# First loads shared between two DMA queues, a prefetch hint for the closing branch, and the last store as one: a softcap attention and feed-forward kernel on one core

## The chip, the cores and the metric

One core of a Trainium2 chip runs the whole kernel. The metric is the device time in microseconds (us) of one execution. A core has TensorE (PE in the rows; its weight loads are PEld), VectorE (DVE), ScalarE (ACT), GpSimd (POOL) and SyncE (SP), which run their own streams of instructions and wait for each other by semaphores. DMAs (copies between the chip's main memory and the on-chip memory) are issued here by SP, ACT and POOL. An engine's letter followed by q (SPq, ACTq) is its sequencer: it issues DMAs, waits, loads registers and branches.

## The reference

```python
def _attn_ref(q, k, v, cap) -> np.ndarray:
    scale = 1.0 / np.sqrt(q.shape[-1])
    scores = scale * np.matmul(q, k.transpose(0, 1, 3, 2))
    scores = cap * np.tanh(scores / cap)
    scores = scores - np.max(scores, axis=-1, keepdims=True)
    attn = np.exp(scores)
    attn = attn / (np.sum(attn, axis=-1, keepdims=True) + 1e-09)
    return np.matmul(attn, v).astype(np.float32)

def _moe_ref(x, w_in, w_out) -> np.ndarray:
    h = x @ w_in
    g = h - np.tanh(h)
    return (g @ w_out).astype(np.float32)
```

q, k and v have 4 batches, 12 heads, 448 rows and 64 columns; the weights are 768 x 2048 and 2048 x 768 and arrive as 64-bit floats. The 1792 x 768 attention result is the input x of the second function.

## The kernel before

The heads are taken in pairs (24 of them: 4 batches times 6). For each pair the kernel loads k and q, transposes them on DVE (L552), splits them into a high and a low part whose products give the precision of 32-bit floats, multiplies on PE (L736 for the first 8 pairs, L701 for the rest), takes tanh and exp on ACT (L746, L709, L801), multiplies with v (L880 and after) and normalises (L912 to L953). The feed-forward part goes over 16 slices of 128 hidden columns: the 64-bit weights are decoded on DVE, split, and used by PE (L1213 to L1215 for the first matrix, L1266 for the second). The last columns of the last rows come in `rest` (L1364 to L1366).

No order is written out by hand. `Build` records each operation with its engine, a cost and a due time in a `Plan`; `Plan.schedule` then plays the program through with these costs and always takes the operation that can start first. `START` holds the times at which PE, ACT, DVE, SP and POOL become free in that play, so it shifts choices all through the order. Copies that ACT or DVE could do (engine "AD") are given out on the way. `Plan.run` tries three settings and emits the instructions in the order of the best.

The places that the change and the prediction touch:

- `softcap_attention_ffn` (L1548): loads `cap`, makes `warm`, a one-element tile, and runs a tanh on it (L1556), which loads ACT's table at the start. Then it builds the main program, loads a flag into a register of every engine (L1575), and branches (L1576): a second, general program stands behind `tc.If(fv == 0)`. With these inputs the flag is 1, so that the general program is jumped over.
- `warm_up` (L474): 18 matmuls on zeros, ahead of the first scores.
- `fetch_qk` (L488): four DMAs for each of k and q, all on SP's queue (L499).
- `fetch_v` (L513): of its two forms, L531 reads a source that stands twice, `tail.unsqueeze(0).to_broadcast([2, TAIL, D])`, so that its outer dimension is 2, into 128 partitions.
- `put` (L1473): stores a tile of results (L1487). The last tile, `fel`, holds rows of two batches, and is stored in halves of 64 partitions. Its last 256 columns, copied out of PSUM last of all, go out in two DMAs, one on SP's queue and one on ACT's.

At the very end SP waits for the landing of every DMA, one semaphore after another, and a barrier of all engines closes the program (L1608).

Of the kernel before, what the change touches and what calls it, by code (L numbers as in the profile page):

```python
# [14 lines left out]
AF = mybir.ActivationFunctionType  # L15
# [35 lines left out]

URGENT = 1000.0

START = (1700.0, 2000.0, 3300.0, 1060.0, 2300.0)
SETTINGS = [(0.0, 0.0), (0.0, 200.0), (0.0, 500.0)]

LAT, LAT_PE, DMA_START, DMA_END = 140.0, 200.0, 650.0, 1100.0
# [34 lines left out]
class Plan:  # L92
# [177 lines left out]
                return c  # L270
        return None

    def run(self, settings):
        best = min((self.schedule(*s) for s in settings), key=lambda r: r[0])
        for o, e in best[1]:
            for b in o.alloc:
                b.tile = self.make(b)
            if o.eng == "AD":
                o.fn(e)
            else:  # L280
                o.fn()
# [33 lines left out]
class Build:  # L315
# [6 lines left out]
    def __init__(self, ctx, tc, q, k, v, w_in, w_out, out, consts, checks, general):  # L322
        self.tc, self.nc = tc, tc.nc
        nc = self.nc
        self.q, self.k, self.v, self.w_in, self.w_out, self.out = q, k, v, w_in, w_out, out
        self.general = general
        self.absc, self.s8 = consts
        self.B, self.H, self.S, self.D = q.shape
        self.NP = self.H // 2
        self.DM, self.DFF = w_in.shape  # L330
        self.ND = self.DM // 128
        self.NF = self.DFF // 128
        self.FULL = self.S // 128 * 128
        self.TAIL = self.S - self.FULL
        B, S, D = self.B, self.S, self.D
        nm = self.nm = "g" if general else "f"
        self.cst = ctx.enter_context(tc.tile_pool(name=nm + "cst", bufs=1))
        self.sb = ctx.enter_context(tc.tile_pool(name=nm + "sb", bufs=2))
        self.ps = ctx.enter_context(tc.tile_pool(name=nm + "ps", bufs=1, space=PSUM))
        self.dram = ctx.enter_context(tc.tile_pool(name=nm + "dram", bufs=1, space=bass.MemoryType.DRAM))  # L340
        self.u_kept = [self.dram.tile([128, 2, self.DM], F32, name=f"{nm}uk{f}") for f in range(self.NF)]
        self.uid = 0
        self.plan = Plan(self.make)
        for name, n in self.sizes().items():
            self.plan.tag(name, n)

        self.fixed = {"kst": [], "kz": [], "kt": [], "vraw": []}  # L350
        S = self.S
        for i in range(self.plan.tags["kst"]):
            t = self.cst.tile([128, 2 * S + self.TAIL], F32R, name=f"{nm}kst{i}")
            nc.gpsimd.memset(t.bitcast(F32)[:, S : S + self.TAIL], 0.0)
            self.fixed["kst"].append(t)


        for i in range(self.plan.tags["kz"]):
            t = self.cst.tile([128, 2 * S], F32R, name=f"{nm}kz{i}")
            nc.gpsimd.memset(t.bitcast(F32)[D:, 0:S], 0.0)  # L360
            nc.gpsimd.memset(t.bitcast(F32)[:D, S:], 0.0)
            self.fixed["kz"].append(t)
        for i in range(self.plan.tags["kt"]):
            t = self.cst.tile([128, 2, 2, self.TAIL], F32R, name=f"{nm}kt{i}")
            nc.gpsimd.memset(t.bitcast(F32)[:D, :, 1, :], 0.0)
            nc.gpsimd.memset(t.bitcast(F32)[D:, :, 0, :], 0.0)
            self.fixed["kt"].append(t)
        self.v1s = {F32: [], F32R: []}
        for i in range(self.plan.tags["vraw"]):
            t = self.cst.tile([128, 4, 2, D], F32, name=f"{nm}vraw{i}")  # L370
            self.fixed["vraw"].append(t)
        tail = B * self.TAIL
        self.xt = [self.cst.tile([128, tail], F32, name=f"{nm}xt{d}") for d in range(self.ND)]
        self.x, self.xt_ops = {}, {d: [] for d in range(self.ND)}
        self.raw_qk, self.ready, self.raw_v = {}, {}, {}
        self.raw, self.u, self.w, self.kept_op = {}, {}, {}, {}
        self.segments = [(m, a, z) for m, a, z in SEGMENTS]
        later = {m for m, a, _ in self.segments if a}
        self.x_kept = {
            m: [self.dram.tile([128, 2, self.FULL], F32, name=f"{nm}xk{m}_{d}") for d in range(self.ND)] for m in later  # L380
        }
        self.y_kept = {
            m: [self.dram.tile([128, self.DM], F32, name=f"{nm}yk{m}_{i}") for i in range(3)] for m in later
        }
        self.x_ops, self.y_ops = {}, {}
        self.acc = {}
        self.at = 0.0
        if not general:
            self.least, self.flagf, self.flag = checks
            self.seen = self.cst.tile([128, 2, self.NF], F32, name="seen")  # L390
            self.ok = self.cst.tile([128, 2, self.NF], F32, name="ok")
            self.bad = self.cst.tile([128, 2], F32, name="bad")
            self.seen_ops = []
# [80 lines left out]
    def warm_up(self):  # L474

        nc, P = self.nc, self.plan.buf("s")
        z = self.plan.buf("xh", [128, self.FULL], F32R)

        def fn():
            for _ in range(WARM):  # L480
                nc.tensor.matmul(P()[:, : self.FULL], z()[:, 0:128], z(), start=True, stop=True)

        o = self.plan.op("D", 300.0, lambda: nc.vector.memset(z().bitcast(F32), 0.0), [], [z], key=-1e6)
        self.plan.op("PE", COLS[384] * WARM, fn, [o], [P], [z], key=-1e6)

    def fetch_qk(self, b, p, np_):  # L488

        nc, S = self.nc, self.S  # L490
        for nm, src in (("k", self.k), ("q", self.q)):
            raw = self.plan.buf(nm + "raw", [128, 2, S // 32, 32])
            ops = []
            for i in range(4):
                hp, dh = divmod(i, 2)
                h = p + self.NP * hp

                def fn(i=i, h=h, dh=dh, raw=raw, src=src):
                    nc.sync.dma_start(  # L499
                        out=raw()[32 * i : 32 * i + 32, 0:np_],  # L500
                        in_=src[b, h : h + np_].rearrange("h (j b) (i a) -> i b h j a", b=32, a=32)[dh],
                    )

                ops.append(
                    self.dma("SP", np_ * S * 128, fn, [], [] if ops else [raw], [raw] if ops else [], slow=2.3)
                )
            for j in range(np_):
                self.raw_qk[nm, b, p + j] = (raw, j, ops)
# [964 lines left out]
    def put(self, i, m, o, deps, cols):  # L1473
        nc, S, T = self.nc, self.S, self.TAIL
        if i < 3:
            r = S * m + 128 * i
            parts = [(slice(0, 128), self.out[r : r + 128, cols])]
        else:

            tails = self.out.rearrange("(b s) c -> b s c", s=S)[2 * (i - 3) : 2 * (i - 3) + 2, self.FULL :, cols]  # L1480
            parts = [(slice(T * j, T * j + T), tails[j]) for j in range(2)]
        for n, (rows, out) in enumerate(parts):

            eng = "A" if i == 4 and n and cols.start else "SP"
            self.dma(
                eng, (rows.stop - rows.start) * (cols.stop - cols.start) * 4,
                lambda q=nc.scalar if eng == "A" else nc.sync, rows=rows, out=out: q.dma_start(  # L1487
                    out=out, in_=o()[rows, cols]
                ),
                deps, [], [o], key=self.at + 20000,  # L1490
            )


    def emit(self):
# [21 lines left out]
        done, b = 0.0, 0  # L1516
# [4 lines left out]
        for c in gen:  # L1521
            if isinstance(c, tuple):
                if c[1] == NP - 1:
                    done, b = 0.0, c[0] + 1
# [8 lines left out]
        done, k = 0.0, 0  # L1533
        self.at = starts[0]
        for c in self.moe():
# [5 lines left out]
                self.at = starts[k] + done * (starts[k + 1] - starts[k]) / own[k]  # L1541
            else:
                self.at = starts[k] + done
        self.plan.run(SETTINGS[:1] if self.general else SETTINGS)


@with_exitstack
def softcap_attention_ffn(ctx: ExitStack, tc: tile.TileContext, q, k, v, cap, w_in, w_out, out):  # L1548
    nc = tc.nc
    cpool = ctx.enter_context(tc.tile_pool(name="consts", bufs=1))  # L1550
    c = cpool.tile([128, 1], F32, name="capt")
    nc.sync.dma_start(out=c, in_=cap.to_broadcast([128, 1]))

    warm = cpool.tile([1, 1], F32, name="warm")
    nc.vector.memset(warm, 0.0)
    nc.scalar.activation(warm, warm, AF.Tanh)  # L1556
    neg = cpool.tile([128, 1], F32, name="negc")
    nc.vector.tensor_scalar_mul(neg, c, -1.0)

    absc = cpool.tile([128, 1], F32, name="absc")  # L1560
# [3 lines left out]
    s8 = cpool.tile([128, 1], F32, name="s8")  # L1564
# [2 lines left out]
    nc.vector.tensor_scalar(flagf, absc[0:1], CAP_BOUND, None, op0=ALU.is_le)  # L1567
    least = cpool.tile([128, 1], F32, name="least")
    nc.vector.memset(least, F64_MIN)
    args = (q, k, v, w_in, w_out, out, (absc, s8), (least, flagf, flag))  # L1570
    with ExitStack() as es:
        build = Build(es, tc, *args, general=False)
        es.enter_context(tc.manual_schedule())
        build.emit()
    fv = nc.values_load(flag[0:1, 0:1], min_val=0, max_val=1)  # L1575
    with tc.If(fv == 0):  # L1576
        with ExitStack() as es:
            build = Build(es, tc, *args, general=True)
            es.enter_context(tc.manual_schedule())
            build.emit()  # L1580
# [32 lines left out]
```

## Time and profile before

| what | us |
|---|---|
| median of 3 runs (lowest, highest) | 705.78 (705.69, 705.79) |
| the profiled execution | 704.82 |
| its span, from the first to the last instruction | 703.0 |
| PE busy in the span | 686.1 |
| ACT busy | 535.6 |
| DVE busy | 520.5 |
| POOL busy | 21.9 |

The profiled execution is one run, recorded by the hardware; its span leaves out 1.82 us that lie around the first and last instruction. Busy time counts an engine's computing instructions, not its sequencer's. Start times in rows count from the start of the span.

### The profile page before, as it was taken

To read this page: it belongs to the slowest core of one execution; us is meant where nothing else is said; L and a number is where in the kernel's file an instruction comes from. 1 tells how busy PE (TensorE), PEld (TensorE's weight loads), DVE (VectorE), ACT (ScalarE), POOL (GpSimd) and SP (SyncE) were. 2 spreads that over 40 slices of the span, in tenths; PEclk is the share of its full clock that TensorE was granted. 3 is DMA by queue.
4 is the path that set the end of the run, shared out by engine and by line. 5 is a ranking of instruction groups with operands and counts; after the bars stand their busy time and mean duration, and the time that the engine had idled before them with its cause. 6 is when DMAs were issued, how large, how long until landed. Compare 5 with 4: busy or idle time off the path is not lost.

```text
span 703.0 us, 10228 instructions
## 1 busy us (share of the span) xinstructions
PE 686.1 (98%) x3672; PEld 587.7 (84%) x3672; DVE 520.5 (74%) x799; ACT 535.6 (76%) x925; POOL 21.9 (3%) x51
## 2 busy tenths in 40 slices
PE   8999999999999999999999999999999999999995
PEld 6445677777889998899989888989999999999995
DVE  4889998999887889998799789798784334333431
ACT  6988878788896959498888998899785555555454
POOL 2011100000000000000000000000000000000000
PEclk9999999999999999999999999999999999999998
DMA  7999999999954646799576865577569544566513
GB/s 107 162 226 243 280 252 243 212 238 260 192 201 147 132 133 188 262 198 323 191 162 190 259 183 149 173 202 217 156 175 269 166 126 135 159 180 179 142 39 118
DMA packets 159520, 133.06 MB, mean 189 GB/s; under 512 B 115748, under 2 KB 144036, under 8 KB 159460
## 3 DMA queue, kind: packets, MB, share of 16 engines
q1 hardware_dynamic: 156308, 117.30, 66.5%
q0 software_dynamic: 3072, 14.94, 5.9%
q8 instruction: 31, 0.51, 0.3%
q14 instruction: 29, 0.24, 0.1%
q10 hardware_dynamic: 80, 0.07, 0.0%
HBM read 110.66 MB, written 21.63 MB: 188 GB/s over the span
## 4 chain that ended last, share of the span: by engine, by line
PE 70%; ACT 12%; DVE 10%; issue 3%; DMA 2%; SPq 2%; DVEq 0%; ACTq 0%
PE facc L1266 22%; PE fh L1213 9%; PE fh L1215 9%; PE fh L1214 9%; PE fs L880 4%; PE fs L701 4%; PE fs L1266 3%; PE fs L882 3%; PE fs L883 2%; PE fs L885 2%; SPq L499 2%; DVE fu L1074 1%; DVE fsumT L912 1%; ACT fe L801 1%; ACT fe L709 1%
## 5 line engine op out<-in xcount | busy, mean ns | idle before, releaser
L1266 PE MATMUL facc<-fwo,fgh 128*128 128x512 f32 (+1 forms) x768 | 167.5, 340 | 0.0
L1266 PEld LDWEIGHTS facc<-fwo,fgh 128*128 128x128 f32 x768 | 123.8, 188 | 15.8 <-issue 2.2
L1213 PE MATMUL fh<-fxh,fwi 128*128 128x384 f32 x384 | 132.8, 346 | 1.1 <-DVE fg L1228 1.1
L1215 PE MATMUL fh<-fxh,fwi 128*128 128x384 f32 x384 | 129.9, 338 | 0.0
L1214 PE MATMUL fh<-fxl,fwi 128*128 128x384 f32 x384 | 128.7, 335 | 0.0
L1266 PE MATMUL facc<-fwo,fgl 128*128 128x512 f32 (+1 forms) x384 | 98.6, 338 | 0.0
L1228 DVE TENSOR_TENSOR fg<-fh,fg 128x384 f32<-128x384 f32 x64 | 35.6, 556 | 64.1 <-ACT fg L1226 63.5
L459 DVE TENSOR_TENSOR fwi<-fu,fwi 128x768 fp32r<-128x768 f32 x66 | 62.9, 953 | 22.3 <-ACT fwi L448 21.4
L1213 PEld LDWEIGHTS fh<-fxh,fwi 128*128 128x128 f32 x384 | 72.1, 188 | 7.0 <-DVE fg L1228 2.6
L448 ACT CAST fwi<-fu 128x768 fp32r<-128x768 f32 x59 | 49.3, 836 | 34.1 <-PE fh L1215 31.1
L1214 PEld LDWEIGHTS fh<-fxl,fwi 128*128 128x128 f32 x384 | 72.2, 188 | 2.1 <-issue 1.3
L1215 PEld LDWEIGHTS fh<-fxh,fwi 128*128 128x128 f32 x384 | 72.0, 187 | 0.0
L459 DVE TENSOR_TENSOR fwo<-fu,fwo 128x768 fp32r<-128x768 f32 x66 | 62.9, 953 | 10.0 <-ACT fwo L448 9.2
L1266 PEld LDWEIGHTS facc<-fwo,fgl 128*128 128x128 f32 x384 | 58.7, 188 | 8.4
L1226 ACT ACTIVATE fg<-fh 128x384 f32<-128x384 f32 x64 | 31.2, 488 | 35.9 <-PE fh L1215 35.6
L709 ACT ACTIVATE fe<-fs 128x448 f32<-128x448 f32 x91 | 46.8, 543 | 10.3 <-PE fs L701 9.6
L801 ACT ACTIVATE fe<-fe,absc 128x896 f32<-128x896 f32 (+1 forms) x52 | 48.8, 954 | 0.3
L448 ACT CAST fgh<-fg 128x384 fp32r<-128x384 f32 x63 | 32.5, 516 | 21.0 <-PE facc L1266 11.1
L701 PE MATMUL fs<-fqst,fkst 128*128 128x448 f32 x128 | 45.9, 379 | 2.2 <-DVE fsumT L912 1.0
L459 DVE TENSOR_TENSOR fgl<-fg,fgh 128x384 fp32r<-128x384 f32 x64 | 35.3, 552 | 15.3 <-ACT fgh L448 14.9
L459 DVE TENSOR_TENSOR fel<-fe,feh 128x896 fp32r<-128x896 f32 x39 | 42.5, 1090 | 5.1 <-ACT feh L448 4.5
L448 ACT CAST fwo<-fu 128x768 fp32r<-128x768 f32 x53 | 44.3, 836 | 1.9
(188 smaller groups left out, 1307.7 us busy)
## 6 DMA issues: line engine op xcount, KB each, us to landing
fu<-fuk SPq DMA_DIRECT2D x48, 768.0 KB
fw<-in_moe_w_in_dram SPq DMA_DIRECT2D x64, 384.0 KB
fw<-in_moe_w_out_dram SPq DMA_DIRECT2D x32, 768.0 KB
fuk<-fu POOLq DMA_DIRECT2D x16, 768.0 KB, 5.9
fqraw<-in_q_dram SPq DMA_DIRECT2D x44, 112.0 KB
fkraw<-in_k_dram SPq DMA_DIRECT2D x44, 112.0 KB
out_dram<-fo SPq DMA_DIRECT2D x12, 384.0 KB
fvraw<-in_v_dram SPq DMA_DIRECT2D x26, 96.0 KB
```

Of the source, the lines that this page charges most:

```text
L448: self.nc.scalar.copy(out(), in_())
L459: lambda: self.nc.vector.tensor_sub(lo(), x(), hi().bitcast(F32)),
L701: nc.tensor.matmul(ps()[:, :S], k, q, start=n == 0, stop=n == passes - 1)
L709: S, lambda: nc.scalar.activation(dst(), ps()[:, :S], AF.Tanh), [o],
L801: lambda e=e, w=w: nc.scalar.activation(e()[:, :w, :], e()[:, :w, :], AF.Exp, scale=self.absc),
L880: nc.tensor.matmul(out, va, e, start=n == 0, stop=n == 3)
L1213: nc.tensor.matmul(h()[:, :n], wh, ah, start=(d == 0), stop=False)
L1214: nc.tensor.matmul(h()[:, :n], wh, al, start=False, stop=False)
L1215: nc.tensor.matmul(h()[:, :n], wl, ah, start=False, stop=(d == ND - 1))
L1226: n, lambda: nc.scalar.activation(g()[:, :n], h()[:, :n], AF.Tanh), [prev], [g], [h], psum=True, key=k
L1228: o = self.dve(n, lambda: nc.vector.tensor_sub(g()[:, :n], h()[:, :n], g()[:, :n]), [o], [], [g, h], key=k + 600)
L1266: nc.tensor.matmul(banks[bk]()[:, c0 : c0 + ne], lhs()[:, ts], w()[:, k, e0 : e0 + ne], start=bk in firsts and bk not in begun, stop=stop ...
```

## The change

It has four parts. `fetch_qk` gives the eight loads of the first pair (batch 0, pair 0) in halves to two queues: the first two of k and of q go to ACT's queue, with a due time that puts them ahead of all else there. The warm-up tanh, and with it ACT's table load, becomes an operation of the plan, due just behind these loads. The `If` gets a label, and `near`, called once the plan comes within 7000 ns of its end, marks the branch as likely taken on ACT, DVE, POOL and SP (not PE). `put` stores the last 256 columns of the last tile as one DMA of 128 partitions on ACT's queue. `START` gets new values.

```diff
-START = (1700.0, 2000.0, 3300.0, 1060.0, 2300.0)
+NEAR = 7000.0
+
+START = (1300.0, 750.0, 800.0, 1060.0, 2300.0)
...
-    def run(self, settings):
+    def run(self, settings, near=None):
         best = min((self.schedule(*s) for s in settings), key=lambda r: r[0])
         for o, e in best[1]:
+            if near and o.end > best[0] - NEAR:
+                near()
+                near = None
...
         self.plan.op("PE", COLS[384] * WARM, fn, [o], [P], [z], key=-1e6)
+        o = self.plan.op("SP", 0.0, lambda: None, key=-9.5e5, lag=2100.0)
+        self.plan.op("D", 900.0, lambda: None, [o], key=-9.5e5)
+        self.plan.op(
+            "A", 1500.0, lambda: nc.scalar.activation(self.warm, self.warm, AF.Tanh), key=-9e5,
+        )
...
-                def fn(i=i, h=h, dh=dh, raw=raw, src=src):
-                    nc.sync.dma_start(
+                eng = "SP" if hp or p or b or self.general else "A"
+                key = -1e6 if eng == "A" else 1e18
+
+                def fn(i=i, h=h, dh=dh, raw=raw, src=src, q=nc.scalar if eng == "A" else nc.sync):
+                    q.dma_start(
...
+        elif cols.start:
+            t = self.out.rearrange("(b s) c -> b s c", s=S)[2 * (i - 3) : 2 * (i - 3) + 2, self.FULL :, cols]
+            parts = [(slice(0, 128), t)]
         else:
...
-            eng = "A" if i == 4 and n and cols.start else "SP"
+            eng = "A" if cols.start else "SP"
...
+    def near(self):
+
+        e = mybir.EngineType
+        self.tc.mark_branch_hint_location("skip", "LikelyTaken", [e.Activation, e.DVE, e.Pool, e.SP])
...
-    nc.scalar.activation(warm, warm, AF.Tanh)
...
-    with tc.If(fv == 0):
+    with tc.If(fv == 0, label="skip"):
```

What the built programs say, at three places. Names are tiles (with f ahead for the main program) and the numbers behind them are buffer numbers; lines of the changed file are higher by up to 23.

The head of SP's queue before:

```order
L1552 DMA capt<-in_cap_dram 128x1
L499 DMA fqraw_134<-in_q_dram 32x14x32 x4
L499 DMA fkraw_139<-in_k_dram 32x14x32 x4
L499 DMA fqraw_165<-in_q_dram 32x14x32 x4
L499 DMA fkraw_175<-in_k_dram 32x14x32 x4
L526 DMA fv1float_194<-in_v_dram 128x3x64 x2
```

and now:

```order
L1631 BRANCH_PREFETCH_HINT
L1576 DMA capt<-in_cap_dram 128x1
L512 DMA fkraw_133<-in_k_dram 32x14x32 x2
L512 DMA fqraw_159<-in_q_dram 32x14x32 x2
L512 DMA fqraw_165<-in_q_dram 32x14x32 x4
L512 DMA fkraw_173<-in_k_dram 32x14x32 x4
L539 DMA fv1float_185<-in_v_dram 128x3x64 x2
```

Of the first pair SP issues four loads in place of eight, k ahead of q, and all that follows moves up by four. The hint, which the source marks near the end of the plan, stands at the head of the program.

The head of ACT before:

```order
L1556 ACT_TABLE_LOAD
L1556 ACTIVATE warm<-warm 1x1
L575 ACTIVATE fqst_170<-fqT_167,s_69 128x448
L448 CAST fkst_103<-fkT_177 128x448
L448 CAST fkt_110<-fkst_103 64x2x64
L575 ACTIVATE fqst_202<-fqT_199,s_69 128x448
```

and now (on DVE the transpose of k likewise stands ahead of that of q, with the low part of k between them):

```order
L1631 BRANCH_PREFETCH_HINT
L512 DMA fkraw_133<-in_k_dram 32x14x32 x2
L512 DMA fqraw_159<-in_q_dram 32x14x32 x2
L493 ACT_TABLE_LOAD
L493 ACTIVATE warm<-warm 1x1
L453 CAST fkst_102<-fkT_169 128x448
L453 CAST fkt_109<-fkst_102 64x2x64 x2
L588 ACTIVATE fqst_183<-fqT_177,s_68 128x448
```

The table load stands behind four issues, and ACT takes k ahead of q.

The end of SP's queue before, up to the branch:

```order
L1487 DMA out_dram<-fo_7082 128x768
L1487 DMA out_dram<-feh_7118 64x768 x2
L1487 DMA out_dram<-fel_7131 64x512 x2
L1487 DMA out_dram<-fel_7131 64x256
L1575 TENSOR_LOAD flag
L1575 ISA x2
L1576 COMPARE_AND_BRANCH
```

and now the end of ACT:

```order
L453 COPY fel_7135<-fs_5711 128x512
L453 COPY fel_7135<-fh_7073 128x256
L1503 DMA out_dram<-fel_7135 2x64x256
L1598 TENSOR_LOAD flag
L1599 COMPARE_AND_BRANCH
```

SP has one store less ahead of its register load; ACT's one store has an outer dimension of 2 where it had 64 partitions of one batch. Between these ends the order of PE differs in its first 820 or so instructions (in the run shown these end near 195 us) and is the same from there on.

## Rows read from the trace of the kernel before

**Rows 1.** The page: busy us of each engine, share of the span, instructions.

```profile
PE 686.1 (98%) x3672; PEld 587.7 (84%) x3672; DVE 520.5 (74%) x799; ACT 535.6 (76%) x925; POOL 21.9 (3%) x51
```

**Rows 2.** Busy us by stretch: length, engines, PEclk, DMA share, GB/s.

```profile
50.00:100.00 50.00, 47.96 (x212) 30.99 (x211) 49.18 (x76) 41.23 (x72) 6.49 (x12) 1.00 1.11 260
200.00:690.00 490.00, 488.42 (x2787) 447.44 (x2786) 346.92 (x525) 366.25 (x628) 3.20 (x6) 1.00 0.63 180
```

**Rows 3.** PE's waits: who for whom, us in total, times, longest.

```profile
PE fh L1213 <- DVE fg L1228: 1.1, 1, 1.1
```

**Rows 4.** Timeline of the start: start us, us, engine, operation [idle before].

```profile
0.73 1.28 ACT L1556 ACT_TABLE_LOAD   x1 [0.73 <-PEq L1595]
1.20 1.97 SPq L499 DMA_DIRECT2D fqraw<-in_q_dram  x4
3.21 2.04 SPq L499 DMA_DIRECT2D fkraw<-in_k_dram  x4
5.14 0.65 DVE L552 STREAM_TRANSPOSE fqT<-fqraw 128x448 f32<-128x448 f32 x1 [1.08 <-DMA fqraw<-in_q_dram]
5.82 0.67 ACT L575 ACTIVATE fqst<-fqT,s 128x448 fp32r<-128x448 f32 x1 [3.59 <-DVE fqT L552]
7.13 0.64 DVE L552 STREAM_TRANSPOSE fkT<-fkraw 128x448 f32<-128x448 f32 x1
7.80 0.56 ACT L448 CAST fkst<-fkT 128x448 fp32r<-128x448 f32 x1 [1.31 <-DVE fkT L552]
8.39 0.62 DVE L459 TENSOR_TENSOR fkst<-fkT,fkst 128x448 fp32r<-128x448 f32 x1 [0.63 <-ACT fkst L448]
8.42 1.24 PE L736 MATMUL facc<-fqst,fkst 64*128 64x448 f32 x6 [1.59 <-ACT fkst L448]
9.05 0.30 ACT L448 CAST fkt<-fkst 64x128 fp32r<-64x128 f32 x1 [0.69 <-DVE fkst L459]
```

**Rows 5.** Busy us by stretch, around PE's first idle time.

```profile
5.88:9.29 3.41, 1.81 (x12) 1.10 (x10) 2.09 (x4) 1.41 (x3) 0.00 (x0) 1.00 0.69 112
9.29:12.70 3.41, 3.41 (x15) 2.34 (x15) 2.58 (x5) 2.75 (x7) 0.00 (x0) 0.50 0.56 109
```

**Rows 6.** Line 1487 after 690 us: ns min/median/max, first, last start.

```profile
L1487 SPq DMA_DIRECT2D out_dram<-fel x3: 537/588/1090, 693.9 to 695.6; - x3
...
L1487 ACTq DMA_DIRECT2D out_dram<-fel x1: 556/556/556, 695.6 to 695.6; - x1
```

**Rows 7.** Timeline of ACT at the end.

```profile
695.22 0.37 ACT L448 COPY fel<-fh 128x256 f32<-128x256 f32 x1 [2.13 <-PE fh L1366]
```

**Rows 8.** Line 1575, the load of the flag.

```profile
L1575 ACTq TENSOR_LOAD <-flag x1: 713/713/713, 696.2 to 696.2; - x1
L1575 SPq TENSOR_LOAD <-flag x1: 927/927/927, 696.8 to 696.8; - x1
```

**Rows 9.** Line 1576, the branch and the semaphores behind it.

```profile
L1576 SPq EVENT_SEMAPHORE  x8: 17/17/17, 700.7 to 701.3; - x8
...
L1576 ACTq COMPARE_BRANCH  x1: 54/54/54, 697.0 to 697.0; - x1
...
L1576 SPq COMPARE_BRANCH  x1: 50/50/50, 698.1 to 698.1; - x1
L1576 ACTq EVENT_SEMAPHORE  x1: 17/17/17, 700.1 to 700.1; - x1
```

**Rows 10.** Busy us by stretch at the end.

```profile
698.00:698.50 0.50, 0.00 (x0) 0.00 (x0) 0.00 (x0) 0.00 (x0) 0.00 (x0) 1.00 0.14 41
698.50:699.00 0.50, 0.00 (x0) 0.00 (x0) 0.00 (x0) 0.00 (x0) 0.00 (x0) 0.78 0.00 0
```

**Rows 11.** Timeline of SP near 308 us.

```profile
308.00 1.14 SPq L531 DMA_DIRECT2D fvraw<-in_v_dram  x2
```

**Rows 12.** DMA view, 310 to 311.2 us: busy tenths in 40 slices.

```profile
DMA  1111111111111111111111111211111111111111
...
DMA packets 165, 0.04 MB, mean 35 GB/s; under 512 B 165, under 2 KB 165, under 8 KB 165
```

**Rows 13.** DMA view, 30 to 40 us: queue, kind, packets, MB, share.

```profile
q14 instruction: 2, 0.02, 0.6%
```

More of the change, by code (lines that the diff above doesn't have):

```diff
@@ L388, in __init__ @@
         if not general:
-            self.least, self.flagf, self.flag = checks
+            self.least, self.flagf, self.flag, self.warm = checks
             self.seen = self.cst.tile([128, 2, self.NF], F32, name="seen")
@@ L504, in fetch_qk @@
                 ops.append(
-                    self.dma("SP", np_ * S * 128, fn, [], [] if ops else [raw], [raw] if ops else [], slow=2.3)
+                    self.dma(eng, np_ * S * 128, fn, [], [] if ops else [raw], [raw] if ops else [], slow=2.3, key=key)
                 )
@@ L1543, in emit @@
                 self.at = starts[k] + done
-        self.plan.run(SETTINGS[:1] if self.general else SETTINGS)
+        if self.general:
+            self.plan.run(SETTINGS[:1])
+        else:
+            self.plan.run(SETTINGS, self.near)
+    def near(self):
+        e = mybir.EngineType
+        self.tc.mark_branch_hint_location("skip", "LikelyTaken", [e.Activation, e.DVE, e.Pool, e.SP])
 @with_exitstack
@@ L1569, in softcap_attention_ffn @@
     nc.vector.memset(least, F64_MIN)
-    args = (q, k, v, w_in, w_out, out, (absc, s8), (least, flagf, flag))
+    args = (q, k, v, w_in, w_out, out, (absc, s8), (least, flagf, flag, warm))
     with ExitStack() as es:
```

## The prediction

> **What bounds the kernel now.** I read the page first: PE is busy 686.1 of 703.0 us, and no other engine more than 76% [rows 1]. The stretches say where this holds: from 200 to 690 us PE is busy 488.42 of 490 us, between 50 and 100 us it shares the limit with DVE, busy 49.18 of 50 [rows 2], and among its waits after the start the longest is 1.1 us [rows 3]. So there is little to win between the first scores and the last matmul, and the change does not touch the work there. What is left lies at both ends, and there I read the timelines.
>
> The start: the first scores begin at 8.42 us, after PE stood idle for 1.59 us. What they wait for is a chain: four issues for q on SP (1.20 to 3.17 us), four for k (3.21 to 5.25), about two microseconds to the landing, k's transpose at 7.13, its high part at 7.80, its low part at 8.39 [rows 4]. An issue takes half a microsecond and the data land one issue after another: the queue's issues set the pace. Right after that idle time the granted clock of PE is 0.50, the lower of its two levels (1.2 GHz for 2.4), for 3.41 us in which PE is busy throughout [rows 5].
>
> The end: ACT's last copy ends at 695.59 us [rows 7]. Then both queues issue a store, ACT in 0.556 us and SP in 1.090 [rows 6]; each loads the flag (ACT at 696.2, SP at 696.8) [rows 8] and branches (697.0 and 698.1). The instruction behind the branch comes at 700.1 on ACT and 700.7 on SP, that is 3.1 and 2.6 us later [rows 9], in which, as I read it, the code at the branch's target is fetched, while the last data were written before 698.5 us [rows 10]. SP's path is the one that ends last, and from its first semaphore (700.7) to the end of the span are 2.3 us.
>
> **The change part by part.**
>
> *Loads.* Four issues leave SP's queue (4 x 0.51 = 2.04 us) and run on ACT's at the same time. SP issues k at about 1.2 and 1.7 us, q at 2.2 and 2.7. From the start of the last issue to the transpose were 2.4 us before (4.8 to 7.13 for k, by four issues in 2.04 us) [rows 4], so k's transpose can start at 4.1 and q's data are there at 5.1. ACT is free for k at 0.73 + 4 x 0.51 + 1.28 (table load) + 0.2 = 4.3 us, so the displaced table load costs nothing: its cover is the wait for k's transpose, until 4.8. Its cover gone, every issue that takes longer counts. Then with the durations and steps of the rows: high part of k at 4.8, low part at 5.4 to 6.0, two casts of 0.30 on ACT until 6.6, q's transpose on DVE 6.0 to 6.7, q's scaling on ACT 6.7 to 7.4, first scores at 7.4 where they began at 8.42: **1.0 us** less. The later loads are 2 us earlier on SP, so they don't take this back. Bounds: -0.8 (a rival below) and 1.6, when PE would start as the warm-up ends (1.59 us of idle gone).
>
> *Clock.* With 0.5 us of idle instead of 1.59 the fall of the clock may not come. Price: between 0 and 1.7 us (half of 3.41) [rows 5]. No row shows how little idle is enough; I take the middle, **0.8 us**, and keep both ends.
>
> *Order in the middle.* The new `START` values change the order until about 195 us. PE's waits there are a few, of up to 1.1 us [rows 3]; they may go or come. I take 0, with 1.5 us on either side.
>
> *Hint.* One instruction at the head of four queues: 0.05 us by the branch rows [rows 9], nothing to speak of. At the branch it can take away up to 2.6 us on SP and 3.1 on ACT. What is late next is the landing of the last store, below. So the hint itself I cost at nothing.
>
> *Last store.* SP has no store after 695.1 us, so it loads the flag there and branches 1.3 us later, at 696.4 (698.1 before); even with a fetch of 2.6 us behind the branch it is at its first semaphore at 699.0 in place of 700.7. ACT without a working hint is done at 700.1 as before, which still leaves the end at 700.9. So by the issue alone, 1.7 us are won and with the hint up to 2.3. But the one store has an outer dimension of 2. The nearest row is L531, whose source has one too: after two such issues [rows 11] the sixteen DMA engines are busy by little more than one tenth, and move 35 GB/s [rows 12], as if two of them worked. Of the same 128 KB the old halves let all work and were in by 698.5 us. At 35 to 49 GB/s (the latter from a larger packet: 1 KB here, 256 bytes there, and 1.4 times is my estimate) 128 KB take 2.7 to 3.7 us; issue until 696.2, some 1.2 us until the first data (L531: its second issue ends at 309.14, and 32 KB at 35 GB/s, 0.9 us, bring it to the 311.2 us up to which the row shows it): landing at 700.1 to 701.1. SP waits for this landing third of eight, 2.1 us before the end: 702.2 to 703.2 for 703.0. I take **0.2 us** less, between -0.9 (30 GB/s, should earlier stores be in the way: a landing at 701.8) and 2.3 (all sixteen engines).
>
> The Trainium skill ("DMA: Bandwidth & Descriptors", Why a DMA increments its semaphore by 16 and not by 1) says that a DMA runs on the largest number up to 16 that divides the outermost dimensions of both sides, which is 2 here. By that rule too the sum loses the 1.7 to 2.3 us that the shorter queue gives; the trace agrees with it at 35 GB/s.
>
> *Sum.* 704.82 - 1.0 - 0.8 - 0.2 = 702.8 us for the profiled execution. The median of the runs lies 0.96 us above that one, so I forecast **703.8 us** as the median.
>
> **The rivals.**
>
> 1. *The queues share what issues.* At 695.6 us both queues issue at once, and SP's takes 1.090 us, 0.53 more than its others of that tile [rows 6]: as if it waited for ACT's 0.556. Against it speaks that this is one place. If so at the start, the eight loads land no earlier, ACT's four issues take 1.09 each, and its table load ends at 0.73 + 4.36 + 1.28 = 6.4; high part of k at 6.6, low at 7.2 to 7.9, casts to 8.5, q's scaling to 9.2, first scores at 9.2: 0.8 later than before, and the clock falls as it did. 704.82 + 0.8 - 0.2 = 705.4, as a median 706.4: no difference. The Trainium skill ("DMA: Bandwidth & Descriptors", Queues, rings and completion order) says that the two queues have no descriptor generator of their own, which is this rival.
>
> 2. *The one store uses all engines.* Then its landing stays before 698.8, the tail gives 1.7 to 2.3, and with 1.0 and 0.8 at the start the median is about 701.9. For it speaks only that the two sides are 128 partitions in all.
>
> 3. *Slower: the hint acts where it stands.* It is the first instruction of four queues, and the branch comes 690 us later. If it makes each queue fetch the far code instead of its own next block, ACT and DVE stand still where they leave their first block; instruction blocks are fetched from 30 us on [rows 13], where the work depends on both. Price: 2.6 to 3.1 us each [rows 9], up to 6.2 together, less the 2.0 of the sum: a median of up to 710. It decides once more than 3.4 us of it reach PE. Against it: buffers between the engines take up part, and one stop alone makes no difference.
>
> 4. *The hint does nothing*, because the block fetched so early is gone by the branch. By the sum this changes nothing, since the store's landing is later than either fetch; without the two-engine landing it would cost 0.6.
>
> **How the numbers follow.** About 0.2% (1.4 us) is what a measurement of this kernel can tell from no change: faster means under 704.4. The forecast (two queues that issue side by side, two DMA engines for the store) has 0.45; with the clock's 0 to 1.7, the store's bounds and the middle's 1.5 it spans 702.0 to 705.6 and is faster in 0.37 of the 0.45, else no change. Rival 1 has 0.28, nearly all of it no change, 0.03 slower. Rival 2 has 0.13, all but 0.01 faster. Rival 3 has 0.06, 0.05 of it slower. Waits that the new order brings have the last 0.08: 0.02 faster, 0.04 the same, 0.02 slower. In all 0.52 faster, 0.38 the same, 0.10 slower. The range 701.7 to 706.6 takes in rival 2's value and rival 1's, and leaves out rival 3.
>
> **What would show it.** Start: issues of 0.48 to 0.56 us on both queues, k's transpose near 4.1 us, first scores near 7.4; issues near 1.0 us and scores after 8.4 are rival 1. Clock: no stretch at 0.50 before 13 us, or one as before. End: SP's branch 1.7 us earlier against the last copy; some 3 us of DMA at a tenth after it, and SP's semaphores standing at the third until it lands. Hint: the instruction behind SP's branch within 0.5 us. A stop of ACT or DVE of 2 us or more between 25 and 60 us with no releaser would be rival 3. The prediction is wrong if the span from the first scores to the last matmul changes by more than 1.5 us, or if the tail after ACT's last copy shrinks by more than 1 us.

## The result, and the profile after

| | median us (lowest to highest, runs) | ratio to before, 95% interval |
|---|---|---|
| before | 705.57 (704.42 to 705.79, 6) | |
| changed | 709.26 (708.13 to 714.07, 6) | 1.0069 [1.0046, 1.0093] |

The change is slower by 3.7 us, against a forecast of 703.8 and outside the range. The ratio takes in every run, so it need not be the quotient of the two medians. The profiled execution of the changed kernel took 714.07 us, the longest of its six, so it shows more than the median loses; its span is 712.2 us.

The page's first row, against [rows 1]: PE has the same 3672 instructions and is busy 4.2 us longer.

```profile
PE 690.3 (97%) x3672; PEld 591.1 (83%) x3672; DVE 519.0 (73%) x797; ACT 535.6 (75%) x927; POOL 22.1 (3%) x51
```

**The end first**, because it divides the loss. ACT's last copy, the branch (L1599) and the store (L1503), and the stretches behind them (columns as in [rows 2]):

```profile
704.38 0.37 ACT L453 COPY fel<-fh 128x256 f32<-128x256 f32 x1 [2.14 <-PE fh L1379]
```

```profile
L1503 ACTq DMA_DIRECT2D out_dram<-fel x1: 1120/1120/1120, 704.8 to 704.8; - x1
```

```profile
L1599 SPq EVENT_SEMAPHORE  x8: 17/17/17, 707.2 to 710.5; - x8
...
L1599 SPq COMPARE_BRANCH  x1: 70/70/70, 705.6 to 705.6; - x1
L1599 ACTq COMPARE_BRANCH  x1: 76/76/76, 706.5 to 706.5; - x1
L1599 ACTq EVENT_SEMAPHORE  x1: 17/17/17, 707.1 to 707.1; - x1
```

```profile
708.00:709.00 1.00, 0.00 (x0) 0.00 (x0) 0.00 (x0) 0.00 (x0) 0.00 (x0) 1.00 0.14 44
709.00:710.00 1.00, 0.00 (x0) 0.00 (x0) 0.00 (x0) 0.00 (x0) 0.00 (x0) 0.67 0.09 32
710.00:711.00 1.00, 0.00 (x0) 0.00 (x0) 0.00 (x0) 0.00 (x0) 0.00 (x0) 0.50 0.00 0
```

The last copy begins 9.16 us later than in [rows 7]. From its end to the end of the span are 7.45 us (712.2 - 704.75), where there were 7.41: the tail is as it was. The hint works: ACT's next instruction comes 0.6 us after its branch, where 3.1 us passed [rows 9]. On SP 1.6 us pass from the branch to the first semaphore; what of this is a fetch and what the wait for a landing, this profile does not tell. And SP's eight semaphores, 0.6 us from first to last in [rows 9], now take 3.3: one of them stands until the store has landed. ACT's issue ended at 705.9, and data move until about 710 with the DMA engines at a seventh to a tenth.

**The start.** The timeline, against [rows 4], and the longest wait of SP up to 8 us:

```profile
0.82 0.97 ACTq L512 DMA_DIRECT2D fkraw<-in_k_dram  x2
...
1.30 0.94 SPq L512 DMA_DIRECT2D fkraw<-in_k_dram  x2
...
1.82 1.03 ACTq L512 DMA_DIRECT2D fqraw<-in_q_dram  x2
2.28 4.17 SPq L512 DMA_DIRECT2D fqraw<-in_q_dram  x6
...
5.37 0.65 DVE L565 STREAM_TRANSPOSE fkT<-fkraw 128x448 f32<-128x448 f32 x1 [1.05 <-DMA fkraw<-in_k_dram]
...
7.19 0.64 DVE L565 STREAM_TRANSPOSE fqT<-fqraw 128x448 f32<-128x448 f32 x1
...
8.75 0.44 PE L749 MATMUL facc<-fqst,fkt 128*128 128x448 f32 x1 [1.74 <-ACT fqst L588]
```

```profile
SPq L512 <- DMA fkraw<-in_k_dram: 1.3, 1, 1.3
```

Seven of the eight first issues run side by side at 0.42 to 0.51 us each. The eighth, the second of q on SP, waits 1.3 us, which the view puts down to the landing of one of k's loads, and begins at 4.0 us; it lies inside the row of six. k's loads are all issued by 2.3 us. Yet k's transpose waits until 5.37 us (q's, first in line before, began at 5.14), and the first scores begin at 8.75, 0.33 later than before. What the DMA engines did from 3 to 4 us, before and now (columns as in [rows 2]):

```profile
3.00:4.00 1.00, 1.00 (x5) 1.00 (x4) 0.60 (x5) 0.00 (x0) 0.87 (x4) 1.00 0.80 126
```

```profile
3.00:4.00 1.00, 1.00 (x5) 1.00 (x4) 0.34 (x3) 1.00 (x1) 0.89 (x4) 1.00 1.30 201
```

More data moves at a time (from 2 to 5 us 0.40 MB for 0.29), but k's and q's loads are now under way together, and the tensor that is needed first is not there sooner.

**The middle** has the other 8.8 us. PE's waits, to be held against [rows 3]; and stretches at the lower clock:

```profile
PE fs L749 <- DVE fsumT L925: 4.3, 1, 4.3
PE fs L714 <- DVE fsumT L925: 3.0, 4, 2.1
```

```profile
9.29:12.70 3.41, 3.32 (x15) 2.46 (x15) 2.26 (x5) 2.63 (x6) 0.00 (x0) 0.55 0.55 108
...
78.00:84.70 6.70, 6.26 (x26) 4.51 (x26) 6.55 (x13) 4.60 (x9) 0.67 (x2) 0.50 1.17 233
...
173.40:176.90 3.50, 3.50 (x12) 3.03 (x12) 3.44 (x5) 0.77 (x2) 0.00 (x0) 0.51 0.50 158
```

The start falls to 1.2 GHz as in [rows 5]. New are two places in the middle, each a wait of PE and a fall behind it. DVE at the first of them, and PE's row behind it:

```profile
75.54 0.65 DVE L565 STREAM_TRANSPOSE fkT<-fkraw 128x448 f32<-128x448 f32 x1 [2.04 <-DMA fkraw<-in_k_dram]
76.11 1.72 DVE L1087 SCALAR_TENSOR_TENSOR fu<-fw,fu 128x1536 uint32<-128x1536 uint32 x1
77.74 1.33 DVE L925 STREAM_TRANSPOSE fsumT<-fs 64x448 f32<-64x448 f32 x2
```

```profile
78.44 0.74 PE L749 MATMUL fs<-fqst,fkst 64*128 64x448 f32 x1 [4.27 <-DVE fsumT L925]
```

The transpose of a later pair's k stands at the head of DVE's queue and waits 2.04 us for its data; a decode step of 1.72 us follows, and only then the two transposes of the sums (`fsumT`), which free the accumulators PE needs. 4.27 us of wait and half of 6.7 at 0.50, then 2.1 and half of 3.5, are 11.5 us as an upper count, for 8.8 to be explained (before has waits of its own).

### The profile page after: what moved, and what is told of

Same layout as the page of the kernel before. It is cut to its first block, busy times and chain, and to the rows that moved or that the text cites. A ratio compares the mean times of both kernels' runs of the same rounds, so it can differ in the third digit from the quotient of the medians.

```text
span 712.2 us, 10223 instructions
## 1 busy us (share of the span) xinstructions
PE 690.3 (97%) x3672; PEld 591.1 (83%) x3672; DVE 519.0 (73%) x797; ACT 535.6 (75%) x927; POOL 22.1 (3%) x51
## 4 chain that ended last, share of the span: by engine, by line
PE 74%; ACT 9%; DVE 7%; DMA 6%; issue 2%; SPq 1%; DVEq 0%; ACTq 0%
PE facc L1279 23%; PE fh L1226 9%; PE fh L1228 9%; PE fh L1227 9%; PE fs L714 5%; PE fs L893 5%; DMA fw<-in_moe_w_in_dram 3%; PE fs L1279 3%; PE facc L749 3%; PE fs L895 3%; PE fs L896 2%; PE fs L898 2%; DMA fkraw<-in_k_dram 2%; ACT fe L722 1%; ACT fe L814 1%
## 5 line engine op out<-in xcount | busy, mean ns | idle before, releaser
L453 ACT CAST fwi<-fu 128x768 fp32r<-128x768 f32 x56 | 46.9, 837 | 37.2 <-PE fh L1228 33.4
L464 DVE TENSOR_TENSOR fwo<-fu,fwo 128x768 fp32r<-128x768 f32 x66 | 62.9, 952 | 11.5 <-ACT fwo L453 10.9
```

The source lines that it names most:

```text
L453: self.nc.scalar.copy(out(), in_())
L464: lambda: self.nc.vector.tensor_sub(lo(), x(), hi().bitcast(F32)),
```

## The experiments

The times are medians. Each ratio is against the kernel before on the same chip, whose median was 705.5 to 705.8 us.

| experiment | us | ratio, 95% interval |
|---|---|---|
| hint alone | 703.04 | 0.9969 [0.9959, 0.9980] |
| split loads alone | 704.68 | 0.9989 [0.9979, 0.9999] |
| new order alone | 708.93 | 1.0053 [1.0041, 1.0066] |
| all edits, old order | 704.97 | 1.0001 [0.9987, 1.0014] |
| hint and one store | 704.72 | 0.9985 [0.9971, 1.0000] |
| hint and split loads | 703.00 | 0.9958 [0.9944, 0.9973] |
| new order, k's transpose moved on DVE | 707.30 | 1.0026 [1.0012, 1.0041] |
| the same, ACT's casts moved too | 708.31 | 1.0046 [1.0027, 1.0066] |
| new order, k's loads first | 709.24 | 1.0057 [1.0037, 1.0077] |
| before, k's transpose moved ahead | 706.25 | 1.0015 [1.0004, 1.0026] |
| changed, DVE and ACT moved near 74 us | 707.48 | 1.0031 [1.0013, 1.0048] |
| the same, and decode moved near 168 us | 709.03 | 1.0060 [1.0039, 1.0081] |
| the same, last store in halves | 707.48 | 1.0022 [1.0009, 1.0035] |
| changed, old START | 710.12 | 1.0062 [1.0048, 1.0077] |

### Which part of the change costs the time

The planner's order and the emitted instructions can be separated: the plan is left as it is, and only what an operation emits is changed. Theory A: the order is the loss. Rivals: B, the hint at the head; C, loads on a second queue.

**Hint alone** (before, with the label and `near`):

```diff
-    with tc.If(fv == 0):
+    with tc.If(fv == 0, label="skip"):
```

> The kernel before with the hint alone (same order of work, loads and stores as before). Theory A (the loss is the re-planned order of the work up to 195 us): the hint costs nothing and SP's branch falls from 2.6 us to about 0.5; the halves of the last store land by 698.5 to 698.8 as before, so the end comes about 2.0 us earlier: ratio 0.997, about 703.6 for 705.6. Theory B (the hint, standing at the head, makes the queues miss code blocks they need): stops of 2 to 3 us on ACT or DVE in the middle, ratio 1.000 to 1.005. If the hint only works where another change has made room for it, 1.000.

```profile
L1589 SPq EVENT_SEMAPHORE  x8: 17/17/17, 698.5 to 699.1; - x8
...
L1589 SPq COMPARE_BRANCH  x1: 70/70/70, 698.0 to 698.0; - x1
```

Theory A's number: 2.5 us faster. SP goes on 0.5 us after its branch, and as the two halves have landed by then, the whole of it is won. Theory B falls.

**Split loads alone** (before's plan, q first):

```diff
-                    nc.sync.dma_start(
+                    (nc.scalar if first else nc.sync).dma_start(
```

> The kernel before with half of the first pair's loads and the table load behind them on ACT's queue, q first as before, nothing else. If the data's rate and not the issue sets the pace, k's last data land near 6.7 us, first scores at 8.0 to 8.5, ratio 0.9995 to 1.000. If the issue sets it (my prediction), first scores near 7.4 and ratio 0.9975 to 0.9985. Theory C (the loads on a second queue delay later loads, and so cause the waits near 74 and 171 us): ratio 1.004 to 1.007.

```profile
5.33 0.65 DVE L556 STREAM_TRANSPOSE fqT<-fqraw 128x448 f32<-128x448 f32 x1 [1.03 <-DMA fqraw<-in_q_dram]
...
8.60 1.14 PE L740 MATMUL facc<-fqst,fkst 64*128 64x448 f32 x6 [1.11 <-ACT fkst L448]
```

q's four issues are over by 2.1 us in place of 3.2, but two queues bring its data no earlier than one (5.33 for 5.14), and the first scores begin as late as before: the issue does not set the pace. The ratio's interval ends just under 1, but **hint and split loads** together are no faster than the hint within their intervals:

```diff
-    with tc.If(fv == 0):
+    with tc.If(fv == 0, label="skip"):
...
+                    (nc.scalar if first else nc.sync).dma_start(
```

> Hint and split first loads, the order of work of before, the last store in two halves on two queues as before. By the single runs (hint 0.9969, loads 0.9989) 0.9958, about 702.6 for 705.5, if the two add up; 0.9969 if the split loads gain nothing.

0.9958 against 0.9969: whether the loads gain a microsecond stays open. This version is the fastest of all, 2.6 us faster than the kernel before.

**New order alone** (the changed kernel's plan; loads on SP, no hint, halves):

```diff
-                def fn(i=i, h=h, dh=dh, raw=raw, src=src, q=nc.scalar if eng == "A" else nc.sync):
+                def fn(i=i, h=h, dh=dh, raw=raw, src=src, q=nc.sync):
```

> The changed kernel's order of work with the instructions of before: all eight first loads on SP's queue, no hint, the last store in two halves. Theory A (the order is the loss): PE waits of 2 us and more near 74 and 171 us with the clock at 0.50 behind them, and a ratio of 1.005 to 1.009, the changed kernel's own 1.007. Theories B and C (the hint or the split loads): no such waits, ratio 0.998 to 1.001.

Timelines of DVE and PE, and the stretch behind:

```profile
74.42 0.65 DVE L565 STREAM_TRANSPOSE fkT<-fkraw 128x448 f32<-128x448 f32 x1 [1.56 <-DMA fkraw<-in_k_dram]
74.99 1.72 DVE L1087 SCALAR_TENSOR_TENSOR fu<-fw,fu 128x1536 uint32<-128x1536 uint32 x1
76.62 1.33 DVE L925 STREAM_TRANSPOSE fsumT<-fs 64x448 f32<-64x448 f32 x2
```

```profile
77.32 0.74 PE L749 MATMUL fs<-fqst,fkst 64*128 64x448 f32 x1 [3.14 <-DVE fsumT L925]
```

```profile
76.40:83.20 6.80, 5.88 (x24) 4.43 (x26) 6.65 (x14) 4.62 (x9) 0.54 (x1) 0.50 1.09 217
```

**All edits, old order** (before's plan, with split loads, hint and the one store):

```diff
+                    (nc.scalar if first else nc.sync).dma_start(
...
+                    lambda: nc.scalar.dma_start(out=tails, in_=o()[:, cols])
...
+    with tc.If(fv == 0, label="skip"):
```

> The reverse: split loads, hint and one store as in the change, but the order of work of before. Theory A: ratio 0.9985 to 1.000 (start -0.3 us at most, tail 0 to -0.3 because the one store lands 4 us after its issue). Theories B and C: 1.004 to 1.007.

```profile
695.29 0.37 ACT L453 COPY fel<-fh 128x256 f32<-128x256 f32 x1 [2.15 <-PE fh L1375]
```

The last copy stands where it stood before (695.22). So the loss is the re-planned order, and no edit: theory A. In the order's own profile the place near 171 us is absent, the one near 74 us is there.

**Hint and one store** prices the store:

```diff
+            if i == 4 and cols.start:
+                f = (lambda: None) if n == 0 else (
+                    lambda: nc.scalar.dma_start(out=tails, in_=o()[:, cols])
+                )
```

> Hint and the one store on ACT's queue, all else as before. My reading (two DMA engines write it, landing about 4 us after the issue): SP stands at its third semaphore until some 700.5 us, the tail is 1.7 to 2.5 us longer than with the hint and the halves, ratio 0.9995 to 1.0015. If one store costs nothing beyond its issue: 0.997 as with the hint alone.

```profile
L1594 SPq EVENT_SEMAPHORE  x8: 17/17/17, 698.5 to 701.7; - x8
L1594 SPq COMPARE_BRANCH  x1: 70/70/70, 696.8 to 696.8; - x1
```

SP branches 1.2 us earlier than with the halves and is through its semaphores 2.6 us later. The one store gives back some 1.5 us of the hint's 2.5: against the median of before on its own chip the hint gives -2.5 us with the halves and -0.9 with the one store. With the loads split as well the same step is 2.1 us (-2.6 with the halves, -0.5 with all edits in the old order).

### What in the order costs it

In the kernel before, DVE takes the sums ahead of the same transpose of k, and does not wait there at all:

```profile
72.42 0.61 DVE L912 STREAM_TRANSPOSE fsumT<-fs 64x448 f32<-64x448 f32 x1
...
76.42 0.58 DVE L552 STREAM_TRANSPOSE fkT<-fkraw 128x448 f32<-128x448 f32 x1
```

**New order, k's transpose moved** behind the sums on DVE (with one decode step, and ACT's casts behind a copy):

```diff
 TENSOR_SCALAR fu<-fw 128x1536
+STREAM_TRANSPOSE fsumT<-fs 64x448 x2
 STREAM_TRANSPOSE fkT<-fkraw 128x448
 SCALAR_TENSOR_TENSOR fu<-fw,fu 128x1536
-STREAM_TRANSPOSE fsumT<-fs 64x448 x2
```

> The kernel with the new order and the instructions of before, in which one transpose of k on DVE (and one step of a decode behind it, and ACT's two casts of it) is moved behind the next two transposes of sums, which PE waits for; all else is the new order. Theory D (the loss is this place: the transpose of k waits for its data at the head of DVE's queue, and the sums behind it hold PE for 3.1 us, whereupon the clock falls for 6.8 us): the wait near 74 us is 1 us or less, no stretch at 0.50 behind it, ratio 1.000 to 1.002 (order alone: 1.0053). Theory E (the loss is spread over many places of the new order): 1.004 to 1.006.

```profile
PE facc L764 <- ACT fel L774: 1.6, 1, 1.6
...
PE fs L764 <- DVE fsumT L940: 0.6, 1, 0.6
```

Half of the order's loss goes, by the middle of the intervals: the wait for the sums is 0.6 us, but ACT's two casts of k now hold the next release (1.6), and the clock still falls for 6.8 us. Between D and E, so ACT's casts were **moved too**, behind the next two ACT instructions:

```diff
-CAST fkz<-fkT 64x448 x2
 ACTIVATE fel<-facc 128x448
 ACTIVATE fel<-fs 128x448
+CAST fkz<-fkT 64x448 x2
```

> The kernel with the new order, the instructions of before and the transpose of k moved, in which ACT's two casts of that k go behind the next two ACT instructions as well (these free the accumulators that PE waits for second). Theory D, widened (the loss is instructions that wait for k at the head of two queues, DVE's and ACT's): no wait of PE over 1.2 us near 75 us, no fall of the clock behind it, ratio 0.999 to 1.001 (with DVE's move alone 1.0026, with neither 1.0053). If a late k itself is what PE runs out of work for, the wait only moves on: 1.002 to 1.003.

In its profile the clock stays at 1.00 from 76.4 to 83.2 us, as hoped; but the ratio, 1.0046, misses the 0.999 to 1.001 expected. That run (713.29) has the second place, and the twelve runs spread from 706.5 to 713.5, so that the ratio can't be told from the last one. The second place, DVE and PE:

```profile
165.61 0.96 DVE L1107 TENSOR_SCALAR fu<-fw 128x1536 uint32<-128x1536 uint32 x1 [4.19 <-DMA fw<-in_moe_w_in_dram]
```

```profile
172.18 0.74 PE L740 MATMUL fs<-fqst,fkst 128*128 128x448 f32 x1 [4.14 <-DVE fsumT L951]
```

The same pattern with another load: a decode at DVE's head waits 4.19 us for weights, the sums stand behind it.

**New order, k's loads first** (two loads of weights go behind k's four on SP's queue):

```diff
-DMA fw<-in_moe_w_out_dram 128x768
...
-DMA fw<-in_moe_w_in_dram 64x6x128
...
 DMA fkraw<-in_k_dram 32x28x32 x4
+DMA fw<-in_moe_w_out_dram 128x768
+DMA fw<-in_moe_w_in_dram 64x6x128
```

> The new order with the instructions of before, in which two loads of weights on SP's queue go behind the four loads of k that stand behind them, so that k's data are asked for two issues earlier. If the weights' place on SP's queue is what makes k late (theory F), the wait near 74 us goes and the ratio is 1.000 to 1.002. If k is late because its own issues wait on this queue, and DVE's order alone decides (theory D), the wait is still 2 us or more, ratio 1.004 to 1.006; PE may then wait for the weights instead.

```profile
72.99 0.96 DVE L1093 TENSOR_SCALAR fu<-fw 128x1536 uint32<-128x1536 uint32 x1 [1.10 <-DMA fw<-in_moe_w_in_dram]
73.86 0.64 DVE L577 STREAM_TRANSPOSE fkT<-fkraw 128x448 f32<-128x448 f32 x1
76.06 1.33 DVE L937 STREAM_TRANSPOSE fsumT<-fs 64x448 f32<-64x448 f32 x2
```

k is in time, the weights are late in its place, and the sums come only 0.6 us earlier (76.06 for 76.62): theory F falls. **The reverse**, one instruction moved in the kernel before:

```diff
+STREAM_TRANSPOSE fkT<-fkraw 128x448
 STREAM_TRANSPOSE fsumT<-fs 64x448
...
-STREAM_TRANSPOSE fkT<-fkraw 128x448
```

> The kernel before with one instruction moved: on DVE the transpose of the same k (third pair of the second batch) goes ahead of the two transposes of sums that it stands behind, as in the changed kernel's order; loads, stores and all else as before. If DVE's place for it is the cause, DVE stands still from about 72.5 us until the data come at 74 to 75 us, PE waits 2.5 us or more in place of 1.1, the clock falls behind it for 3.4 to 6.8 us, and the ratio is 1.003 to 1.007. If k comes later only in the changed order, PE's wait stays near 1.1 us and the ratio is 0.999 to 1.001.

```profile
74.25 0.65 DVE L562 STREAM_TRANSPOSE fkT<-fkraw 128x448 f32<-128x448 f32 x1 [1.13 <-DMA fkraw<-in_k_dram]
74.82 0.61 DVE L924 STREAM_TRANSPOSE fsumT<-fs 64x448 f32<-64x448 f32 x1
```

```profile
77.01 0.47 PE L748 MATMUL fs<-fqst,fkst 64*128 64x448 f32 x1 [0.66 <-DVE fsumT L924]
```

k's data are as late here (74.25 us), so the lateness was there before and was hidden by DVE's order. One instruction in another place costs about 1 us (0.3 to 1.8 by the interval), with 0.66 us more of wait and a fall of the clock at 77.8 us. That is less than I expected: six matmuls of the feed-forward part stand on PE here as a reserve, and in the new order none.

### Mending the changed kernel

**DVE and ACT moved near 74 us**, by the two edits above (DVE's and ACT's):

```diff
+STREAM_TRANSPOSE fsumT<-fs 64x448 x2
 STREAM_TRANSPOSE fkT<-fkraw 128x448
...
+CAST fkz<-fkT 64x448 x2
```

> The changed kernel with the same few instructions moved on DVE and ACT near 74 us, nothing else. If the place near 74 us is all that the new order loses, 0.999 to 1.001 (705 to 706 us): the tail and the start of the change are worth about nothing together. If the wait near 171 us that its profile showed comes in most of its runs too, 1.002 to 1.004.

1.0031 for 1.0069: by the middles of the intervals the moves win about half of the loss, not all. Nor is the place quite mended by them: in this profile PE still waits 1.2 us for ACT near 77 us, and the clock is at 0.50 from 80 to 83 us. **Decode moved near 168 us as well**:

```diff
 TENSOR_TENSOR fkst<-fkT,fkst 64x448
-TENSOR_SCALAR fu<-fw 128x1536
...
-SCALAR_TENSOR_TENSOR fu<-fw,fu 128x1536
...
 STREAM_TRANSPOSE fsumT<-fs 64x448
+TENSOR_SCALAR fu<-fw 128x1536
+SCALAR_TENSOR_TENSOR fu<-fw,fu 128x1536
```

> The changed kernel with the few instructions near 74 us moved on DVE and ACT, and near 168 us two decode steps on DVE moved behind the two transposes of sums that PE waits for. If the second place is what made the slowest runs (its wait was 4.1 us in one profile and is absent in others), no run is over 708.5 us, and the ratio is 1.000 to 1.002 (1.0031 without). If something else makes these runs, the spread stays at 705.7 to 711.7 us.

```profile
PE fs L749 <- ACT fqst L486: 1.7, 1, 1.7
```

A miss: the slow runs stay (up to 712.4). The late decode makes a wait of its own: ACT waits 2.49 us for it until 172.78, its casts behind come late, and PE waits 1.7 us for one of them, until 175.14. With the **store in halves**:

```diff
-                lambda q=nc.scalar if eng == "A" else nc.sync, rows=rows, out=out: q.dma_start(
+                    y.dma_start(out=z, in_=o()[w, cols]) for y, z, w in (
+                        ((nc.sync, out[0], slice(0, T)), (nc.scalar, out[1], slice(T, 2 * T)))
```

> The same, and the last store in two halves of 64 partitions on two queues as before, with the hint kept. By the price of the one store (hint with it 0.9985, hint without it 0.9969, so 1.1 us or more) 0.998 to 1.000; 0.9958, the best so far, only if the new order with both places mended is as good as the old one.

707.48 for 709.03: the store's price once more, some 1.5 us. The ratio, 1.0022, misses the 0.998 to 1.000 expected. The same edits in the old order (hint and split loads) were 2.6 us faster than before, these are 1.9 us slower, so the moved order still costs 4.5 us here: these moves did not mend it.

**Old START** with all edits: the planner finds a third order.

```diff
-START = (1300.0, 750.0, 800.0, 1060.0, 2300.0)
+START = (1700.0, 2000.0, 3300.0, 1060.0, 2300.0)
```

> The changed kernel with the five START values of before: the planner then finds a third order (DVE's rows differ from both). If the loss belongs to one unlucky order, this one may give anything from 0.997 to 1.007; about 1.000 if it has no such wait, as the start and the tail come to about nothing together. If every order with the loads moved to ACT loses, 1.004 or more.

```profile
72.04 0.65 DVE L565 STREAM_TRANSPOSE fqT<-fqraw 128x448 f32<-128x448 f32 x1 [4.95 <-DMA fqraw<-in_q_dram]
```

```profile
PE fs L749 <- DVE fsumT L925: 5.9, 1, 5.9
```

Again near 74 us, with q's transpose at the head of DVE's queue in the place of k's. Part of this loss lies at the start, though: the first scores begin at 10.17 us, 1.75 later than before, and ACT's last copy at 701.26, 6.0 later. So the new values of `START` are not needed for such a loss: both orders that the planner made from the changed plan (loads and table load moved) put an instruction that waits for data ahead of the sums. Which of these edits brings it, and why, was not tried; that it counts an issue on SP as 0.55 us, where these four of k took 6.59 us in the changed kernel, is a reason only argued.

## Why the prediction was wrong

*Order in the middle: 0 with 1.5 on either side.* This is the step that failed. It measured 3.4 us by the medians (1.0053, order alone), and my own sign for it came: from the first scores to the last copy the profile has 8.8 us more, where more than 1.5 was to prove me wrong. I bounded it by the waits of the order that was there, "of up to 1.1 us" [rows 3]; but the longest wait of one order bounds nothing in another. The row that spoke for more I had quoted myself: from 50 to 100 us the DMA share is 1.11 and DVE is busy 49.18 of 50 [rows 2]. Where the loads are late and DVE has no slack, an order decides by what it puts ahead of the sums. And the price of a wait left out its second half, the fall to 1.2 GHz that I had priced at the start. "Waits that the new order brings" had a chance of 0.08, 0.02 of it slower.

*Loads: -1.0.* Seven of the eight issues did run on two queues side by side, against rival 1. What failed first is the 2.4 us "from the start of the last issue to the transpose": k's last issue began near 1.8 us, its transpose at 5.37, which is 3.6. And that "the queue's issues set the pace" was a misreading of [rows 4]: k's transpose, at 7.13, shows no wait for data there, because DVE was busy with q's low part until 7.21.

```profile
6.53 0.68 DVE L580 SCALAR_TENSOR_TENSOR fqst<-fqT,s,fqst 128x448 fp32r<-128x448 f32 x1 [0.74 <-ACT fqst L575]
```

From the first transpose to the first scores pass 3.28 us before, 3.27 with split loads alone and 3.38 in the changed kernel. So the landing of the first tensor and the chain behind it set the start, and neither got shorter. By itself the part measured -0.8 us [-1.5, -0.1], as a median, without earlier scores in its profile.

The Trainium skill ("DMA: Bandwidth & Descriptors", Queues, rings and completion order) says that each DMA engine takes packets in turn from all queues that have work for it. The trace agrees as far as it goes: with two queues 201 GB/s for 126 from 3 to 4 us, and the first tensor no earlier.

*Clock: -0.8.* It fell as before, after 1.74 us of idle. The step, that less idle time may spare the fall, has no support: with split loads alone PE stood idle for 1.11 us, and the clock was at 0.50 from 11 to 15 us; with the hint alone (timeline and stretch) PE stood idle longer and the clock stayed at 1.00 behind it. Nor was anything of that left at the end: ACT's last copy (third row) begins there at 695.21, for 695.22 in [rows 7].

```profile
8.52 1.14 PE L741 MATMUL facc<-fqst,fkst 64*128 64x448 f32 x6 [2.21 <-ACT fkst L453]
```

```profile
8.10:11.50 3.40, 2.75 (x15) 1.45 (x15) 2.19 (x5) 2.07 (x5) 0.00 (x0) 1.00 0.69 124
```

```profile
695.21 0.37 ACT L453 COPY fel<-fh 128x256 f32<-128x256 f32 x1 [2.14 <-PE fh L1371]
```

*Hint: nothing; last store: 0.2 less.* Together nearly right: the tail is 7.45 us for 7.41, because the store lands 4.2 us after its issue. The 49 GB/s in that term came from a factor of 1.4 that no row shows; the stretches behind the changed kernel's store show 44 and 32. Apart, the hint is worth -2.5 us and the one store +1.5 to +2.1. I wrote that with the hint "up to 2.3" would be won but for the store.

The Trainium skill ("DMA: Bandwidth & Descriptors", Why a DMA increments its semaphore by 16 and not by 1) gives two engines for an outer dimension of 2; a DMA share of 0.14 and 0.09 of sixteen agrees again.

*Rivals 2, 3 and 4* are refuted: the store doesn't use all engines, the hint at the head stops nothing (0.9969), and it works at the branch 700 us later. Rival 1 had the first scores after 8.4 us, and so they came, but not by its mechanism: only one of the eight issues waited.

What stays open: about half of the order's loss is left when k's transpose is moved (1.0026 of 1.0053), the further moves did not lower it, and the second place, seen in two of the profiles, comes and goes from run to run. That it makes the slowest runs is argued from these two and not shown. So the order is shown to be the loss; of the places in it, only the one near 74 us is shown by a move to be a part.

## What to carry to other kernels

An edit that makes a planner replan is two changes; freeze the order, emit the edit into it, and price the two apart: here the edits' best part won 2.5 us and the replan lost more. Where the DMA engines are full, look along each in-order queue for instructions that wait for data ahead of ones the bound engine waits for, and price such a wait with the clock that falls behind it. A store whose outer dimension is 2 cost 1.5 to 2.1 us more here than its two halves.

## What the runs showed of the hardware that I had not expected

- A hint that stands at the head of the program cuts the stop behind the taken branch to 0.5 us on SP (hint alone) and 0.6 on ACT (changed kernel), 700 us later (2.6 and 3.1 without).
- After a like idle time at the start the granted clock fell in some executions (1.74 us, 0.55; with split loads alone 1.11 us, 0.50 from 11 to 15 us) and not in another (2.21 us, 1.00).
- With the first eight loads (56 KB each) on two queues the first tensor landed no earlier than on one (transposes at 5.33 and 5.37 us for 5.14), though 201 GB/s moved from 3 to 4 us in place of 126.
- With the loads split, SP's fourth issue waits 1.3 us (split loads alone and changed kernel); on one queue none of the eight waits. What holds it was not tried.
